# A fused Fourier layer and gated MLP on one core: transposing each half of a tile's rows in one run of four, with the spectral work's plan times moved

## The chip, the cores and the metric

One core of one Trainium2 chip runs the whole program. The metric is the device time of one execution in microseconds (us); the kernel before is given as the median of three runs. One further execution was taken with the hardware profiler, and all rows below come from it. PE is TensorE (matmuls), PEld its weight loads, DVE is VectorE, ACT is ScalarE, POOL is GpSimd and SP the engine that issues most of the DMAs.

## The reference

```python
X = np.fft.rfft(x, axis=1)                       # x: 8 x 3072 x 256
Yr = Xr @ w_r - Xi @ w_i + b_r
Yi = Xr @ w_i + Xi @ w_r + b_i
Y  = softshrink(Yr, 0.01) + 1j * softshrink(Yi, 0.01)
y  = np.fft.irfft(Y, n=3072, axis=1)             # 24576 rows of 256
xn = y / sqrt(mean(y*y) + 1e-6) * rms_g
out = (silu(xn @ w_gate) * (xn @ w_val)) @ w_out # d_ff = 1536
```

## The kernel before, in words

There are eight batches of 3072 rows. Each batch goes through the **spectral work** (a DFT of 3072 points split into 24 x 128, a 256 x 256 mixing product, soft threshold, and the way back) and then through the **MLP**. The spectral work of batch b+1 runs beside the MLP of batch b; that of batch 0 stands alone at the start.

The MLP works on tiles of 512 rows: six per batch, 48 in all, numbered T = 0 to 47. Each tile goes through 12 **steps**, one per block of 128 of the 1536 hidden columns, so a batch is 72 steps. A step makes the gate and value products (`straight`, line 949, for T below 3, and `products`, line 973, with seven products instead of eight, from T = 3 on), the silu and the multiplication on ACT and DVE, and the product with w_out (`down`, line 1016) that adds up in the PSUM bank `acc` over the 12 steps. Every operand is held as two rounded halves (high and low), and each product is three matmuls of 128 x 128 by 128 x 256. All matmuls of the steady part (lines 959, 983, 1018 of the MLP, 572, 611 to 634, 676 to 699 of the spectral work) have this one shape, and come in groups of three or a multiple of it.

**The transposes** (`transposes`, line 912; the matmuls are line 917). Before a tile's first step, its 512 x 256 normalised rows must stand with the 256 columns on the partitions: eight transposes of 128 x 128 per tile on TensorE, four for each half h of the columns. The four of one half go to one PSUM bank of the ring `f`, which has a single bank and which the spectral products `pf`, `pm` and `pb` also take in turn; ACT then copies the bank to `xf` (line 935) or, for T below 3, ACT and DVE copy it to `xn` (lines 930 and 932). For T above 3 the first half (h = 0) is emitted as two pairs: `cut` is 2, a pair is issued, then an operation on a made-up engine "D" that emits nothing and costs 0.8 in the plan, then the other pair. The second half (h = 1) is one run of four. For T = 1 to 3 both halves are runs of four. T = 0 takes its rows from a separate tile.

**What sets the order.** `Plan` (line 128) collects operations with engines, a cost, the tokens they read and write and a due time `at[0]`, counted in steps. `ordered` (line 147) hands out the rooms of each ring in order of due time; `schedule` (line 190) simulates the engines, forward by due time and then, eight times, backward and forward by how late an operation may start, and keeps the best. The instructions are emitted in that order, and each engine works in the order of emission. The constants of lines 35 to 40 are due times: `LATER` (line 1024) is how many steps after its own a step's w_out product is due; `DECODE` (line 1172) moves the decoding of the weight groups 1 to 5, each with one load issued by SP (`weights64`, line 843), two ACT and four DVE operations, and the splitting and storing behind them; `FIRST` and `LATER_ON` (line 1283) say between which steps the three parts of the spectral work of batch 1 and of batches 2 to 7 are spread (lines 1265 to 1275), the table loads of POOL (`load_tab`, line 544) among them; `BACK` is added to all of those.

Of the kernel before, what the change touches and what calls it, by code (L numbers as in the profile page):

```python
# [31 lines left out]
ORDER = [0, 9, 6, 3, 8, 4, 10, 2, 1, 7, 5, 11]  # L32
LAM = 0.01
PLAIN_OF = ()
LATER = 4.67
AHEAD = 60
DECODE = (-7.78, -3.84, -1.42)
BACK = -0.5
FIRST = (21.23, 29.83, 51.87, 60.24)
LATER_ON = (-0.73, 5.35, 42.8, 75.89)  # L40
PLAIN = 3
GE = 9

# [254 lines left out]
def fourier_glu_kernel(ctx: ExitStack, tc: tile.TileContext, x, w_r, w_i, b_r, b_i, wg, wv, wo, rg, tabs, units, tws, out):  # L298
    nc = tc.nc
    B, S, D = x.shape  # L300
    FF = wg.shape[1]
    P = 128
# [35 lines left out]
    def f32(ap):  # L338
        return ap.bitcast(F32)
# [7 lines left out]
    def op(engines, cost, fn, r=(), w=()):  # L347
        plan.add(at[0], engines, cost, fn, [*r, *gate], w)

    def dve(n):  # L350
        return 0.09 + n / 990

    def act(n, more=0.0):
        return 0.1 + more + n / 1180
# [39 lines left out]
    class Bank(Room):  # L394
# [9 lines left out]
        def flat(self):  # L404
            return self().rearrange("p a b -> p (a b)")
# [11 lines left out]
    def load_x(s, n=4):  # L417
        if s.b:
            op("S", 0.01, lambda _: s(), [], s.tok(*range(24)))
        for p in (0, 4, 2, 6)[:8 // n]:  # L420
            for a in range(3):
                slots = range(8 * a + p, 8 * a + p + n)

                def go(_, slots=slots):
                    for p0, p1 in _runs(slots[0], slots[-1] + 1):
                        nc.sync.dma_start(out=s()[:, p0:p1, :], in_=xv[s.b][:, N1[p0]:N1[p1 - 1] + 1:3, :])

                op("S", 2.4 * n / 4, go, [], s.tok(*slots))
# [483 lines left out]
    def transposes(get, toks, T, h, xn, xf):  # L912
        ps = Room("acc" if T == 0 and h else "f", (P, 4, P), f"pt{T}_{h}")

        def go(i0, i1):
            for i in range(i0, i1):
                PE.matmul(  # L917
                    ps()[:, i, :], lhsT=get(i)[:, h * P:(h + 1) * P], rhs=ident,
                    start=(i == 0), stop=(i == 3), is_transpose=True, skip_group_check=True,
                )  # L920

        flat = lambda: ps().rearrange("p a b -> p (a b)")
        cut = 2 if T > PLAIN and not h else 4
        op("P", 0.45 * cut / 4, lambda _: go(0, cut), toks, ps.first)
        if cut < 4:
            op("D", 0.8, lambda _: None, [], [ps.tok])
            op("P", 0.25, lambda _: go(cut, 4), toks, [ps.tok])
        if xf is None:
            to = lambda lp: xn()[:, lp, 2 * h:2 * h + 2, :].rearrange("p a b -> p (a b)")
            op("A", act(512) + 0.09, lambda _: A.activation(to(0), flat(), AF.Copy, scale=rgs[:, h:h + 1]), [ps.tok, "rgs"], [xn.part(f"h{h}0")] + xn.first * (h == 0))  # L930
            w = [xn.part(f"h{h}1")] + ["ready"] * (T == 0 and h)
            op("V", dve(512) + 0.06, lambda _: V.scalar_tensor_tensor(to(1), flat(), rgs[:, h:h + 1], f32(to(0)), ALU.mult, ALU.subtract), [ps.tok, xn.part(f"h{h}0")], w)
            return
        to = lambda: xf()[:, 2 * h:2 * h + 2, :].rearrange("p a b -> p (a b)")
        op("A", act(512) + 0.09, lambda _: A.activation(to(), flat(), AF.Copy, scale=rgs[:, h:h + 1]), [ps.tok, "rgs"], [xf.tok] + xf.first * (h == 0))

    def combine(T, xn, xf):
        x = [(lambda k=k: xf()[:, k, :]) for k in range(7)]
        for o, a, b, f in ((4, 1, 3, ALU.add), (1, 0, 1, ALU.subtract), (5, 4, 0, ALU.subtract), (6, 2, 5, ALU.subtract)):
            add(256, lambda e, o=o, a=a, b=b, f=f: e(x[o](), x[a](), x[b](), f), [], [xf.tok])  # L940
        for k0, k1 in ((0, 2), (4, 6), (2, 4), (6, 7)):
            w = [xn.part(f"h{k0}")] + xn.first * (k0 == 0)
            q = lambda k0=k0, k1=k1: xf()[:, k0:k1]
            op("A", act(256 * (k1 - k0)), lambda _, q=q, k0=k0, k1=k1: A.activation(xn()[:, 0, k0:k1], q(), AF.Copy), [xf.tok], w)
            add(256 * (k1 - k0), lambda f, q=q, k0=k0, k1=k1: f(xn()[:, 1, k0:k1], q(), f32(xn()[:, 0, k0:k1]), ALU.subtract), [xf.tok], w)
# [56 lines left out]
    def step(n, xn, i, mixed):  # L1002
# [20 lines left out]

        at[0] = n + LATER
        for c in range(4):
# [3 lines left out]
    def store(b, t, o):  # L1029
        r = Room("o", (P, 4, D), f"o{b}_{t}")  # L1030
        for k in range(2):
            op("A", act(512), lambda _, k=k: A.activation(r()[:, 2 * k:2 * k + 2], o()[:, 2 * k:2 * k + 2], AF.Copy), [o.tok], [r.tok] if k else r.first)

        def go(_):
            for p0, p1 in _runs(4 * t, 4 * t + 4):
                nc.sync.dma_start(out=ov[b][:, N1[p0]:N1[p1 - 1] + 1:3, :], in_=r()[:, p0 - 4 * t:p1 - 4 * t, :])

        op("S", 1.5, go, [r.tok], [])
# [71 lines left out]
    def bits(g, c):  # L1110
        n = 3 * g + c
        get, tok = (lambda: early()[:, n % 6]), early.tok(*range(4 * (n % 6), 4 * (n % 6) + 4))
        op("S", 2.4, lambda _: weights64(g, c, get()), [], tok)
        w = decode(g, c, get, tok, ("h", "h") if n == 2 else (("G", "xs"), ("z", "F"))[n % 2])
        if c == 0:
            gate_w[0] = w
        elif c == 1:
            up_weights(g, gate_w[0], w)
        else:
            out_weights(g, w)  # L1120
# [44 lines left out]
    for h in range(2):  # L1165
        transposes(lambda i: rows()[:, i, :], [f"{rows.tok}.{p}" for p in range(4)] + [rows.tok, "ident"], 0, h, xns[0], None)

    for g in range(1, NG):
        if g == GE:
            gate.append("ready")  # L1170
        for c in range(3):
            at[0] = 2 * g + DECODE[c]
            bits(g, c)
# [41 lines left out]
    def spectrum(s, times):  # L1215
# [50 lines left out]
        for k in range(3):  # L1266
# [3 lines left out]
            for m, c in zip(mine, cost):  # L1270
                t = times[k] + (times[k + 1] - times[k]) * done / whole
                o = plan.ops[m]
                pace = (f"go{int(t - AHEAD)}",) if t >= AHEAD else ()
                plan.ops[m] = (t + BACK, *o[1:4], o[4] + pace, o[5])
                done += c

    for b in range(B):
        s = seqs[b]
        if b + 1 < B:
            seqs[b + 1] = Seq(b + 1)  # L1280
            at[0] = STEPS * (b - 1) + 60 if b else 10.6
            load_x(seqs[b + 1])
            spectrum(seqs[b + 1], [STEPS * b + t for t in (FIRST if b == 0 else LATER_ON)])
        for t in range(NT):
            T = b * NT + t
            for i in range(NF):
                n = NF * T + i
                if T:
                    at[0] = n - 3
                    if not plain(T):  # L1290
                        trs[n] = fetch(0, i, Room("tr", (P, 2, 512), f"tr{n}", F32R))
                    else:
                        trs[n] = trs[n - 1] if i % 4 else fetch(2, i // 4, Room("tr", (P, 2, 512), f"tb{n}", F32R))
                    if NF <= n < NF * PLAIN and n % (PLAIN - 1) == 0:
                        at[0] = n - 2.9
                        mixed_weights((n - NF) // (PLAIN - 1))
                    at[0] = n - 1
                    wo_s[n] = fetch(1, i, Room("wo", (P, 2, D), f"wo{n}", F32R))
                o = step(n, xns[T], i, not plain(T))
                if i == 0 and T + 1 < NT * B:  # L1300
                    nb, nt = (b, t + 1) if t + 1 < NT else (b + 1, 0)
                    xns[T + 1] = Room("xn", (P, 2, 7, 256), f"xn{T + 1}", F32R)
                    xf = Room("xf", (P, 7, 256), f"xf{T + 1}") if not plain(T + 1) else None
                    for h in range(2):
                        at[0] = NF * (T + 1) - 4 + h
                        transposes(
                            lambda i, nb=nb, nt=nt: seqs[nb]()[:, 4 * nt + i, :],
                            seqs[nb].tok(*range(4 * nt, 4 * nt + 4)), T + 1, h, xns[T + 1], xf,
                        )
                    if xf:  # L1310
                        combine(T + 1, xns[T + 1], xf)
            at[0] = NF * (T + 1) + LATER - 0.95
            store(b, t, o)
# [31 lines left out]
```

## Time and profile before

| | us |
|---|---|
| median of three runs | 2746.87 |
| lowest and highest run | 2743.99, 2752.15 |
| the profiled execution's own time | 2750.04 |
| its span, first to last instruction | 2748.3 |
| mean granted TensorE clock | 0.996 of full speed |

The span is what the rows add up to; the profiled execution's own time is 1.7 us longer, for what lies around the span. It is 3.2 us (0.1%) above the median of the runs.

How to read the rows. A busy time is the union of an engine's instructions. A matmul row gives the duration of one, start to modelled end, which is longer than the distance from one start to the next, since matmuls are pipelined. A window's "(x59)" counts the instructions that lie in it wholly or in part. PEclk is the granted clock of TensorE as a share of full speed.

### The profile page before, as it was taken

The numbers are of one execution on the slowest core, as the hardware profiler recorded it, in microseconds if no ns is written. First come the engines' busy times: TensorE is split into PE (matmuls) and PEld (weight loads), VectorE is DVE, ScalarE is ACT, GpSimd is POOL, SyncE is SP. The second block draws the span as 40 slices with busy tenths as digits, with TensorE's granted clock in tenths as the row PEclk, the third lists the DMA queues.
The fourth block names the chain that finished last, engine by engine and source line by source line (L and its number), as shares of the span: only waits on it lengthen the run. The fifth ranks groups of instructions, "written<-read, shape, count | busy, mean of one in ns | idle before, by whom it ended". The sixth has DMA issues, their size and how long they took to land.

```text
span 2748.3 us, 60168 instructions
## 1 busy us (share of the span) xinstructions
PE 2710.2 (99%) x23321; PEld 2696.1 (98%) x23321; DVE 2322.3 (84%) x4066; ACT 1982.6 (72%) x4891; POOL 90.4 (3%) x177
## 2 busy tenths in 40 slices
PE   7899999999999999999999999999999999999999
PEld 6799999999999999999999999999999999999999
DVE  9989789987998779987899878997789987976665
ACT  4655678777777778777786777877778777776665
POOL 0000000000000000000000000000000000000000
PEclk9999999999999999999999999999999999999999
DMA  6466667676777767767776676766667676666665
GB/s 216 154 223 215 207 220 252 221 230 218 227 253 225 220 221 231 233 226 219 226 254 222 219 226 216 263 215 224 226 222 259 204 230 218 212 205 221 215 218 186
DMA packets 256112, 610.94 MB, mean 222 GB/s; under 512 B 24401, under 2 KB 81106, under 8 KB 255826
## 3 DMA queue, kind: packets, MB, share of 16 engines
q1 hardware_dynamic: 231634, 519.00, 56.7%
q0 software_dynamic: 24192, 88.09, 10.8%
q8 instruction: 183, 3.00, 0.4%
q14 instruction: 103, 0.84, 0.1%
HBM read 567.68 MB, written 39.32 MB: 221 GB/s over the span
## 4 chain that ended last, share of the span: by engine, by line
PE 96%; DVE 2%; DMA 1%; issue 0%; ACT 0%; SPq 0%; ACTq 0%; DVEq 0%
PE acc L1018 28%; PE v L983 27%; PE g L983 20%; PE pf L572 4%; PE pm L634 4%; PE pm L630 2%; PE pb L699 2%; PE pt L917 2%; PE v L959 2%; PE g L959 1%; PE pm L755 1%; PE pb L694 1%; PE pf L733 1%; PE pb L779 1%; PE pm L611 1%; PE pb L676 0%
## 5 line engine op out<-in xcount | busy, mean ns | idle before, releaser
L1018 PE MATMUL acc<-wo,hs 128*128 128x256 f32 x6912 | 1002.5, 278 | 1.9 <-DVE hs L1011 0.8
L1018 PEld LDWEIGHTS acc<-wo,hs 128*128 128x128 f32 x6912 | 884.8, 188 | 2.7 <-DVE hs L1011 1.0
L983 PE MATMUL v<-xn,tr 128*128 128x256 f32 x4860 | 784.0, 279 | 1.3 <-DVE y L996 1.2
L983 PEld LDWEIGHTS v<-xn,tr 128*128 128x128 f32 x4860 | 657.1, 188 | 2.2 <-DVE y L996 1.9
L983 PE MATMUL g<-xn,wb 128*128 128x256 f32 x3240 | 540.7, 278 | 0.0
L996 DVE TENSOR_TENSOR y<-v,p 128x512 f32<-128x512 f32 x540 | 370.8, 687 | 130.2 <-PE v L983 124.8
L1011 DVE TENSOR_TENSOR hs<-h,hs 128x512 fp32r<-128x512 f32 x576 | 394.9, 686 | 81.0 <-ACT hs L1010 77.6
L1010 ACT ACTIVATE hs<-h 128x512 fp32r<-128x512 f32 x576 | 362.0, 628 | 119.6 <-DVE h L1000 63.5
L983 PEld LDWEIGHTS g<-xn,wb 128*128 128x128 f32 x3240 | 446.4, 188 | 0.3
L1000 DVE TENSOR_TENSOR h<-h,y 128x512 f32<-128x512 f32 x540 | 369.8, 686 | 50.6 <-ACT h L999 47.7
L989 ACT ACTIVATE v<-g 128x256 f32<-128x256 f32 x540 | 199.4, 369 | 132.4 <-PE g L983 128.9
L983 PE MATMUL g<-xn,tr 128*128 128x256 f32 x1620 | 274.6, 278 | 0.0
L983 PE MATMUL v<-xn,wb 128*128 128x256 f32 x1620 | 273.7, 278 | 0.0
L992 ACT ACTIVATE v<-v 128x256 f32<-128x256 f32 x540 | 199.9, 371 | 91.0 <-PE v L983 87.5
L999 ACT ACTIVATE h<-v 128x256 f32<-128x256 f32 x540 | 206.5, 382 | 61.9 <-PE v L983 59.0
L997 ACT ACTIVATE h<-g 128x256 f32<-128x256 f32 x540 | 206.3, 382 | 57.3 <-PE g L983 36.7
L983 PEld LDWEIGHTS g<-xn,tr 128*128 128x128 f32 x1620 | 225.3, 188 | 0.1
L983 PEld LDWEIGHTS v<-xn,wb 128*128 128x128 f32 x1620 | 225.2, 188 | 0.0
L545 POOL DMA_DIRECT2D tab<-in_tabs_dram x168 | 89.4, 532 | 2247.4 <-PE pf L572 1180.2
L990 ACT ACTIVATE p<-g 128x256 f32<-128x256 f32 x300 | 114.2, 381 | 40.7 <-DVE y L996 39.8
L572 PE MATMUL pf<-tab,as 128*128 128x256 f32 x1008 | 134.9, 277 | 0.3 <-issue 0.2
L572 PEld LDWEIGHTS pf<-tab,as 128*128 128x128 f32 x1008 | 123.8, 188 | 0.7 <-issue 0.4
(172 smaller groups left out, 3531.9 us busy)
## 6 DMA issues: line engine op xcount, KB each, us to landing
tr<-dt SPq DMA_DIRECT2D x540, 512.0 KB, 4.0
wo<-do SPq DMA_DIRECT2D x564, 256.0 KB, 3.5
tab<-in_tabs_dram POOLq DMA_DIRECT2D x168, 512.0 KB, 4.5
out_dram<-o SPq DMA_DIRECT2D x32, 512.0 KB, 5.4
seq<-in_x_dram SPq DMA_DIRECT2D x28, 512.0 KB, 6.2
seq<-in_x_dram SPq DMA_DIRECT2D x25, 256.0 KB, 4.7
unit<-in_units_dram SPq DMA_DIRECT2D x12, 512.0 KB, 4.3
dt<-tw SPq DMA_DIRECT2D x12, 512.0 KB, 5.7
```

The lines of the kernel that those rows point to most:

```text
L572: PE.matmul(ps[:, h, :], lhsT=r()[:, lp, ri, h * P:(h + 1) * P], rhs=f[:, rp, ri, :], start=(h + k + ri == 0), stop=(k == 2 and ri == 1), ...
L983: PE.matmul(dst(), lhsT=w(lp), rhs=xn()[:, rp, x, :], start=start and k == 0, stop=k == 2, skip_group_check=True)
L989: op("A", act(256), lambda _: A.activation(left(), p1(), AF.Copy), [one.tok], two.first)
L990: op("AV", {"A": act(256), "V": dve(256)}, lambda e: A.activation(p5(), p5_(), AF.Copy) if e == "A" else V.tensor_copy(p5(), p5_()), [one. ...
L992: op("A", act(256), lambda _: A.activation(right(), left(), AF.Copy), [], [two.tok])
L996: op("V", dve(512), lambda _: V.tensor_tensor(y(), two(), p5().unsqueeze(1).to_broadcast([P, 2, 256]), ALU.add), [two.tok, p5.tok], y.first)
L997: op("A", act(256), lambda _: A.activation(s()[:, :256], p1(), AF.Silu), [one.tok], s.first)
L999: op("A", act(256), lambda _: A.activation(s()[:, 256:], right(), AF.Silu), [two.tok], [s.part("b")])
L1000: op("V", dve(512), lambda _: V.tensor_tensor(s(), s(), y().rearrange("p a b -> p (a b)"), ALU.mult), [y.tok, s.part("b")], [s.tok])
L1010: op("A", act(512), lambda _: A.activation(h()[:, 0], s(), AF.Copy), [s.tok], h.first)
L1011: add(512, lambda f: f(h()[:, 1], s(), f32(h()[:, 0]), ALU.subtract), [s.tok], [h.tok])
L1018: PE.matmul(o()[:, c, :], lhsT=h()[:, lp, c * P:(c + 1) * P], rhs=wo_()[:, rp, :], start=(i == 0 and k == 0 and c % 2 == 0), stop=(i == NF ...
```

## The change

Both halves of each tile are now transposed in one run of four; the two pairs, and the planned pause between them, are gone. For T = 1 to 3 nothing is different in this function, as `cut` was 4 there. Six planning constants have other values.

```diff
-LATER = 4.67
+LATER = 4.77
 AHEAD = 60
-DECODE = (-7.78, -3.84, -1.42)
-BACK = -0.5
-FIRST = (21.23, 29.83, 51.87, 60.24)
-LATER_ON = (-0.73, 5.35, 42.8, 75.89)
+DECODE = (-6.74, -4.23, -1.63)
+BACK = -0.63
+FIRST = (17.81, 28.26, 48.79, 59.49)
+LATER_ON = (-3.72, 6.26, 39.96, 69.5)
...
-        def go(i0, i1):
-            for i in range(i0, i1):
+        def go(_):
+            for i in range(4):
                 PE.matmul(
                     ps()[:, i, :], lhsT=get(i)[:, h * P:(h + 1) * P], rhs=ident,
                     start=(i == 0), stop=(i == 3), is_transpose=True, skip_group_check=True,
                 )
...
-        cut = 2 if T > PLAIN and not h else 4
-        op("P", 0.45 * cut / 4, lambda _: go(0, cut), toks, ps.first)
-        if cut < 4:
-            op("D", 0.8, lambda _: None, [], [ps.tok])
-            op("P", 0.25, lambda _: go(cut, 4), toks, [ps.tok])
+        op("P", 0.45, go, toks, ps.first)
```

## Rows read from the trace of the kernel before

**Rows 1.** The page, part 1: busy time, share of the span and instructions of each engine.
```profile
PE 2710.2 (99%) x23321; PEld 2696.1 (98%) x23321; DVE 2322.3 (84%) x4066; ACT 1982.6 (72%) x4891; POOL 90.4 (3%) x177
```
**Rows 2.** Waits of TensorE, longest first: us in total, times, longest.
```profile
PE warm L1082 <- DMA seq<-in_x_dram: 11.6, 1, 11.6
PE pt L917 <- ACT rows L822: 11.0, 1, 11.0
PE pf L733 <- DVE seq L464: 2.9, 1, 2.9
...
```
**Rows 3.** Windows, TensorE alone: stretch, us, PE busy (count), PEclk, DMA share, GB/s.
```profile
0.00:118.00 118.00, 91.65 (x507) 0.93 0.65 211
118.00:343.00 225.00, 220.56 (x1887) 1.00 0.61 198
343.00:2690.00 2347.00, 2345.05 (x20469) 1.00 0.69 226
2690.00:2748.30 58.30, 52.98 (x466) 0.97 0.54 182
```
**Rows 4.** The chain that ended last: start, us, what (merged).
```profile
33.35 3.45 PE pm L755 x16
...
241.20 1.36 PE pf L572 x12
...
258.15 1.41 PE pf L572 x12
```
**Rows 5.** Windows between the runs of transposes of T = 1 to 4.
```profile
144.10:150.50 6.40, 6.40 (x59) 1.00 0.75 259
151.50:171.40 19.90, 19.90 (x178) 1.00 0.80 254
172.10:185.90 13.80, 13.80 (x120) 1.00 0.60 201
186.70:194.70 8.00, 8.00 (x71) 1.00 0.92 332
239.40:243.60 4.20, 4.20 (x39) 1.00 0.72 212
244.40:334.40 90.00, 90.00 (x766) 1.00 0.63 203
...
353.10:361.20 8.10, 8.10 (x74) 1.00 0.52 174
```
**Rows 6.** Windows between the runs of the last two tiles.
```profile
2615.00:2630.30 15.30, 15.30 (x133) 1.00 0.63 221
...
2635.20:2661.00 25.80, 25.80 (x230) 1.00 0.63 215
2661.50:2676.80 15.30, 15.30 (x132) 1.00 0.69 232
...
2681.70:2741.00 59.30, 59.30 (x526) 1.00 0.59 200
```
**Rows 7.** The transposes' tile pt: duration ns min/median/max, first and last start.
```profile
L917 PE MATMUL pt<-ident,seq x376: 270/272/273, 143.3 to 2681.2; 128*128 128x128 f32 x188
L935 ACT ACTIVATE xf<-pt,rgs x90: 663/682/701, 239.5 to 2681.7; 128x512 f32<-128x512 f32 x90
```
**Rows 8.** Timeline of TensorE at a pair and at a run of four: start, us.
```profile
2630.41 0.38 PE L917 MATMUL pt<-ident,seq 128*128 128x128 f32 x2
...
2630.98 0.75 PE L983 MATMUL v<-xn,tr 128*128 128x256 f32 x5
...
2634.52 0.60 PE L917 MATMUL pt<-ident,seq 128*128 128x128 f32 x4
...
2635.31 0.50 PE L1018 MATMUL acc<-wo,hs 128*128 128x256 f32 x3
```
**Rows 9.** The page, part 6: DMA issues, count, KB each, us to landing.
```profile
tab<-in_tabs_dram POOLq DMA_DIRECT2D x168, 512.0 KB, 4.5
seq<-in_x_dram SPq DMA_DIRECT2D x28, 512.0 KB, 6.2
```

## The prediction

> **What bounds the kernel now.** I read four views, in this order. The page's busy times come first: TensorE is busy for 99% of the span, DVE for 84%, ACT for 72% [rows 1]. The waits of TensorE say whether that is real: its longest three, 25.5 us together, belong to the start, where the first rows land and the first tile is normalised [rows 2]. The windows then show that from 343 to 2690 us it sits idle for only 2347.00 - 2345.05 = 1.95 us [rows 3]. So nothing that another engine does sooner can shorten this stretch; only the number of TensorE's instructions, and the distance from one to the next, can.
>
> That distance has **two values**, and this is what the reader should see. In the chain of work that ended last, the same twelve `pf` matmuls take 1.36 us at 241 us and 1.41 us at 258 us [rows 4]: 113.3 and 117.5 ns each. The windows give it more finely. A matmul's modelled duration (276 to 281 ns) reaches back over the edge of a window, so a window counts about 2.4 too many; 90.00 us with 766 matmuls is 90.00/763.6 = 117.8 ns [rows 5], and 59.30 us with 526 is 113.3 ns [rows 6]. I call them the fast and the slow pace: 113.3 and 117.8 ns, 4.5 ns apart. The granted clock reads 1.00 in all these windows, DMA share and bytes are alike, and no wait stands there: neither the clock nor a late operand makes the slow pace. What changes at the edges of these windows is a **run of transposes** [rows 5, 6].
>
> How much is slow: 20469 matmuls at 113.3 ns would need 2319.8 us (113.33 taken) of the 2347.0 [rows 3]. The difference is 27.2 us, 1.95 of it idle; the other 25.2 us, at 4.5 ns each, are 5,600 slow matmuls, 27% of the stretch. (Transposes count as matmuls here; the next part shows that they cost about the same.)
>
> **The change part by part.**
>
> *The transposes themselves.* 376 of them serve T = 1 to 47 [rows 7], before and after. From the start of a pair to the fourth matmul start behind it 0.57 us pass, of which three matmul distances at the slow pace are 0.353: the pair costs 0.22. A run of four: 0.79 less three fast distances, 0.34, is 0.45 [rows 8]. Two pairs or one run: 0.44 against 0.45, 44 times, is nothing (-0.5 to +0.5 us).
>
> *The bank.* Before, ACT could copy the first half only after the second pair, some 15 us after the first pair in the last tiles (15.3 us is the slow window between them) [rows 6]. Now it can do so right behind the run, in 0.68 us [rows 7], so ring `f` comes free sooner for the spectral products. Those do not hold TensorE up in the steady part, whose idle time is 1.95 us in all [rows 3]; taken as 0, with -2 us as the most it could give. The planned pause emits no instruction: 0.
>
> *The pace behind each run.* This is the term that decides. There are 44 tiles with two runs of four each in place of a pair, a pair and a run. What the trace shows:
> - A pair met at the fast pace leaves the slow one: the last two tiles have 133 and 132 matmuls in 15.3 us between their pairs, where the fast pace would give 137 [rows 6].
> - The run of four that ends such a tile leaves the fast pace: 230 in 25.8 us and 526 in 59.3 us [rows 6], as it does at T = 4 [rows 5]. All 44 do so in the timeline, of which the first and the last windows are shown.
> - But none of these 44 runs follows a run of four; a pair is always in between. Runs of four alone are shown only by T = 1 to 3. A window's count tells the pace: after the six runs, 59 (fast would be 58.9, slow 56.7), 178 (178, 171), 120 (124, 119.5), 71 (73, 70.3), 39 (39.5, 38) and 766 (797, 766) [rows 5]: fast, fast, slow, slow, fast, slow. The fourth run met the slow pace and left it; the fifth came behind a stall of the start. The last slow stretch lasts 90 us, until a pair and a run of four come.
>
> So the nearest rows for the new pattern, runs of four behind runs of four, end slow in three of six cases. The bounds are: every run ends fast, 0 slow matmuls, -25.2 us; every run ends slow, 20469 x 4.5 = 92.1 us, +66.9 us. I take half, by those six: 10,234 x 4.5 = 46.1 us, less the 25.2 paid now, **+20.9 us**.
>
> The Trainium skill, page "TensorE: Matmul & The Clock Gate", section "LDWEIGHTS (loading the stationary operand)", gives the time of a weight load by its columns alone, about 128/1.2 = 107 ns by my estimate, whatever ran before. By that rule there is one pace, and this term is 0 instead of +20.9. The two paces at a clock of 1.00 speak against it [rows 5], but it is a rival below.
>
> *The moved plan times.* `LATER` puts each w_out product 0.1 step later, and with it the stores, issued by SP, by 0.1 step: an order of work among products that are all waiting, 0. `DECODE` moves, for weight groups 1 to 5, the load on SP's queue, two ACT and four DVE operations and the splitting behind them by +1.04, -0.39 and -0.21 step; `FIRST` starts the next batch's spectral work 3.42 steps sooner. Both fall in the stretch from 118 to 343 us, where TensorE is idle for 225.00 - 220.56 = 4.4 us [rows 3]. All of that gone is -4.4; as much again is +4.4; nothing in the rows says which, so 0. `LATER_ON` and `BACK` start the spectral work of batches 2 to 7 about 3 steps sooner and end it 6.5 steps sooner. Its table loads go out on POOL's queue (168 of them, landing in 4.5 us), and the loads of x on SP's keep their due time [rows 9]. DVE and ACT have 16% and 28% to spare [rows 1], and the cover is that TensorE always has MLP products ready; were it gone, the price is the fourth rival's. 0.
>
> **The sum.** 2750.0 (the profiled execution) + 20.9 = 2770.9. That execution lies 3.2 us over the median of the runs, so on the median's scale 2767.7, say **2768 us**.
>
> **The rivals.**
>
> *Every run of four ends fast* (the other side: faster). For it: all 44 runs of four from T = 4 on do, from either pace, and 25.8 and 59.3 us at 113.3 ns follow in the last two tiles [rows 6]. If what matters is the run's own length, and T = 1 to 3 are disturbed by the start, then taking the pairs away takes the slow stretches away. It shows from where under 18% of the matmuls are slow (18% is 16.6 us, 8.6 less than now). Time: 2750.0 - 25.2 = 2724.8, on the median's scale 2722. Against it: the slow stretch of 90 us that began behind a run of four with no stall before it [rows 5]. Chance 0.30.
>
> *Nothing changes.* Either the pace is not the transposes' doing, or the new mixture is again near 27% slow (18 to 36%: -9 to +8 us). Time 2747. The change not doing what it says belongs here too: the four are issued by one function call, so they cannot be drawn apart, but with one bank in ring `f` the second run still waits for ACT's copy of the first, and the two halves may end up as they were. Chance 0.12.
>
> *The clock falls behind a longer run.* At the start, where the granted clock averages 0.93 over 118 us [rows 3], sixteen matmuls took 3.45 us, 216 ns each [rows 4], the lower level of 1.2 GHz, twice the 113.3. If each of the 88 runs of four and the three matmuls behind it, 0.79 us [rows 8], went at that level, each would take 0.79 us longer, +70 us: 2750.0 + 70 - 3.2 = 2817. Against it: 50 runs of four stand in this trace and the clock reads 1.00 from 118 to 2690 us [rows 3]. Chance 0.01.
>
> *The spectral work's earlier start makes DVE late at a batch's edge.* The next batch's first sums would then stand in DVE's queue ahead of the MLP's multiplications while a load of x, 6.2 us, is under way [rows 9]. Six edges x 6.2 us is +37 us at most: 2784. It decides once TensorE's waits on DVE at 343 us and every 330 us after sum to over 8 us; they are under 2 now [rows 3]. Chance 0.04.
>
> **How the numbers follow.** The forecast, that a good part of the runs of four leave the slow pace, has 0.53. About 0.3%, 8 us, is what a measurement of this kernel can tell from no change. Slower by more: 0.53 + 0.01 + 0.04 = 0.58. Faster by more: 0.30. Within: 0.12. The forecast begins at 37% slow: 34.1 - 25.2 = +8.9, on the median's scale 2756. At 83% slow it is 76.4 - 25.2 = +51.2, there 2798, and 2800 with 2 for the plan times. So its own range is 2756 to 2800. The range for 8 in 10 takes in the fast rival and the first 2 us of its plan-time bound: 2720 to 2800; the clock and the all-slow end (2814) are left out.
>
> **What would show it.** Right: windows between the runs of the last tiles with 117.8 ns between matmuls, also behind runs of four; TensorE's count per 330 us falling; mean matmul durations nearer 281 than 276 ns; clock 1.00; waits as now. Wrong: 113.3 ns from run to run (then the fast rival), or new waits of TensorE on DVE at the edges of batches.

## The result and the profile after

The changed kernel takes **2774.27 us** (median of 4 runs, 2773.16 to 2775.29) against 2747.74 for the kernel before (4 runs): 26.5 us more, a ratio of 1.0096 with a 95% interval of 1.0078 to 1.0113. The forecast was 2768, with a range of 2720 to 2800. The profiled execution of after took 2773.16 us, its span is 2771.4.

Busy times of after (the page, part 1), the line that answers to [rows 1]:

```profile
PE 2733.7 (99%) x23321; PEld 2720.0 (98%) x23321; DVE 2330.5 (84%) x4063; ACT 1987.4 (72%) x4894; POOL 90.4 (3%) x177
```

TensorE issues the same 23321 matmuls and is busy 23.5 us longer: that is the whole growth of the span (2771.4 - 2748.3 = 23.1). Its waits in after, in the columns of [rows 2]:

```profile
PE warm L1078 <- DMA seq<-in_x_dram: 11.6, 1, 11.6
PE pt L917 <- ACT rows L822: 11.0, 1, 11.0
PE pf L733 <- DVE seq L464: 2.2, 1, 2.2
PE pf L572 <- ACT as L564: 1.5, 1, 1.5
...
PE acc L1014 <- ACT o L1028: 0.7, 4, 0.2
```

The two longest are equal and none of the others is long enough to matter. The last line shown is new, 0.7 us in four waits: at four edges between batches the first w_out product waits for the copy of the bank `acc`. The windows of TensorE in after, in the columns of [rows 3]:

```profile
0.00:118.00 118.00, 91.64 (x524) 0.96 0.66 211
118.00:343.00 225.00, 221.02 (x1901) 0.99 0.62 202
343.00:2690.00 2347.00, 2344.87 (x20239) 1.00 0.69 224
```

The third line is the result. In the same 2347 us TensorE is as busy as before (2344.87 against 2345.05 us), at the same clock and with the same DMA share, and finishes 230 matmuls fewer. I call **slow time** what a kernel's busy time in this stretch has over 113.33 ns for each matmul counted: 2344.87 - 20239 x 0.11333 = 51.2 us here, 25.3 us before [rows 3]. It has grown by 25.9 us. At 4.5 ns each that is 11,400 slow matmuls, 56% of them, where there were 27%. Slow time also holds what a wait costs beyond the idle time that the profile shows, because a matmul's modelled duration (276 ns) reaches 163 ns past the next start: at the wait of 0.18 us at 1106.62 us in after, two distances are 455 and 223 ns, 0.45 us more than two fast ones. So a share of slow matmuls worked out "by the row" is an upper figure; counted one by one from the starts in the trace, 55% of the distances are at the slow pace in after and 25% before.

Windows between the runs of four of the last tiles of after, in the columns of [rows 6]:

```profile
2543.30:2589.80 46.50, 46.50 (x413) 1.00 0.68 227
2590.60:2609.60 19.00, 19.00 (x164) 1.00 0.64 222
2610.40:2637.30 26.90, 26.90 (x231) 1.00 0.58 202
2638.20:2656.40 18.20, 18.20 (x163) 1.00 0.68 229
2657.20:2684.10 26.90, 26.90 (x230) 1.00 0.62 211
2684.90:2704.00 19.10, 19.10 (x165) 1.00 0.64 211
2704.90:2764.00 59.10, 59.10 (x524) 1.00 0.60 201
```

With 2.4 taken from each count, as in the prediction, the distances are 113.2, 117.6, 117.7, 113.3, 118.2, 117.5 and 113.3 ns. Two stretches at about 117.8 ns follow one at 113.3 ns, then one at 113.3 ns comes again: **each run of four here moves the pace on by one place in a cycle of three**. In [rows 6] a pair began a slow stretch and the run of four behind it ended it; here a slow stretch lasts from one run of four to the next but one.

The transposes' own rows in after, in the columns of [rows 7], show that they did not change:

```profile
L917 PE MATMUL pt<-ident,seq x376: 270/272/273, 142.4 to 2704.4; 128*128 128x128 f32 x188
L931 ACT ACTIVATE xf<-pt,rgs x90: 671/690/709, 246.1 to 2704.8; 128x512 f32<-128x512 f32 x90
```

### The profile page after: what moved, and what is told of

The parts are those of the page before. It is cut to its first block, busy times and chain, and to the rows that moved or that the text cites. A ratio compares the mean times of both kernels' runs of the same rounds, so it can differ in the third digit from the quotient of the medians.

```text
span 2771.4 us, 60161 instructions
## 1 busy us (share of the span) xinstructions
PE 2733.7 (99%) x23321; PEld 2720.0 (98%) x23321; DVE 2330.5 (84%) x4063; ACT 1987.4 (72%) x4894; POOL 90.4 (3%) x177
## 4 chain that ended last, share of the span: by engine, by line
PE 97%; DVE 2%; DMA 1%; ACT 1%; issue 0%; SPq 0%; ACTq 0%; DVEq 0%
PE acc L1014 28%; PE v L979 27%; PE g L979 20%; PE pf L572 4%; PE pm L634 4%; PE pb L699 2%; PE pm L630 2%; PE v L955 2%; PE g L955 2%; PE pt L917 2%; PE pm L755 1%; PE pb L694 1%; PE pb L779 1%; PE pm L611 1%; PE pf L733 1%
```

## The experiments

Each line of windows below is TensorE's from 343 to 2690 us, in the columns of [rows 3], and each slow time is worked out from it as above. A measured ratio is against the kernel before, measured beside it, with its 95% interval.

**1 and 2: the shape and the plan times, one at a time.** The first keeps the runs of four and puts the six planning constants back; the second keeps the new constants and puts the pairs back.

```diff
...
-FIRST = (17.81, 28.26, 48.79, 59.49)
-LATER_ON = (-3.72, 6.26, 39.96, 69.5)
+FIRST = (21.23, 29.83, 51.87, 60.24)
+LATER_ON = (-0.73, 5.35, 42.8, 75.89)
...
```

> The kernel before with the runs of four alone; the plan times stay the old ones. Theory A (the runs' shape sets the pace: met by runs of four alone, the pace goes fast, slow, slow, fast from run to run): 45 to 65% of the matmuls at 117.8 ns, 2762 to 2785 us. Rival B (the moved plan times cost the 26 us): 27% slow as before, 2740 to 2755 us.

Measured: 2781.08 us, ratio 1.0122 (1.0106 to 1.0138).

```profile
343.00:2690.00 2347.00, 2341.23 (x20141) 1.00 0.68 223
```

```diff
...
-        op("P", 0.45, go, toks, ps.first)
+        cut = 2 if T > PLAIN and not h else 4
+        op("P", 0.45 * cut / 4, lambda _: go(0, cut), toks, ps.first)
+        if cut < 4:
+            op("D", 0.8, lambda _: None, [], [ps.tok])
+            op("P", 0.25, lambda _: go(cut, 4), toks, [ps.tok])
```

> The changed kernel's plan times with the old pairs. Theory A: 25 to 32% of the matmuls slow, 2740 to 2757 us. Rival B: 2766 to 2782 us, or waits of TensorE that the kernel before does not have.

Measured: 2756.17 us, ratio 1.0030 (1.0017 to 1.0044).

```profile
343.00:2690.00 2347.00, 2343.00 (x20452) 1.00 0.69 226
```

The slow time is 58.7 us with fours and the old times, 25.2 with pairs and the new times. So theory A's ranges hold in both, and B's in neither: the shape of the runs makes the loss, +33 us of slow time by itself (with it the plan also orders the other matmuls anew; experiment 3 does not). The plan times then took 6.8 us off again (2781.08 to 2774.27): with the runs in other places the slow time is 51.2 instead of 58.7 us, and idle time 2.1 instead of 5.8. With pairs the new times cost 9 us at the median. The row explains 2 of these (idle 4.00 against 1.95 us, a few short waits, far from the 26 us that B needed); the profiled execution took 2753.42, and the seven runs spread from 2749.30 to 2758.87, so the rest stays open.

**3: runs of six.** The first two transposes of each run are written twice from T = 1 on, 188 more in all.

```diff
-            for i in range(4):
+            run = ([0, 1, 2, 3] * 3)[:2] * (T > 0)
+            for k, i in enumerate(run + [0, 1, 2, 3]):
...
```

> The changed kernel with two transposes written twice, so that every run of T = 1 to 47 is six long: 188 more transposes at 0.11 us are +21 us. Theory A in its sharper form (each transpose moves the pace on by one of three places, so a run moves it by its length modulo three): a run of six leaves the pace that it meets, the pace changes only at stalls, the slow 53 us go; 2740 to 2755 us and under 15% slow. Rival C (any run of some length upsets the pace, two of three behind it are slow): 2790 to 2800 us.

Measured: 2751.99 us, ratio 1.0020 (1.0010 to 1.0030).

```profile
343.00:2690.00 2347.00, 2344.18 (x20586) 1.00 0.69 226
```

188 transposes were added, 20.5 us at 109 ns each, and the kernel is 22.3 us faster than after. The slow time fell to 11.2 us. This settles that the transposes steer the pace: nothing else was touched. In the trace the other 22,937 matmuls of TensorE stand in the same order as in after, and the runs at the same places among them; the same holds for experiments 6, 7, 10 and 12. That the count goes modulo three was the theory of this moment; the next runs ended it.

**4 and 5: all eight in one run, with one repeated (nine) and without (eight).** The second half's four go to a bank of the ring `gb`, and the run is placed eight steps later in the listing. The diff is of the eight; the nine has `* 1` for `* 0`.

```diff
+            work = [(h, i) for i in range(4)] if not T else [(0, 0)] * 0 + [(k, i) for k in range(2) for i in range(4)]
+            for m, (k, i) in enumerate(work):
...
-        op("P", 0.45, go, toks, ps.first)
+        if not T:
+            op("P", 0.45, go, toks, ps.first)
+        elif not h:
+            op("P", 0.9, go, toks, banks[0].first + banks[1].first)
...
-                if i == 0 and T + 1 < NT * B:
+                if i == NF - 4 and T + 1 < NT * B:
...
+                    banks = [Room(tag, (P, 4, P), f"pt{T + 1}_{k}") for k, tag in enumerate(("f", "gb"))]
```

> The changed kernel with all eight transposes of a tile of T = 1 to 47 in one run into two banks, and one written twice: runs of nine, 47 more transposes, +5 us. Theory A, sharper form: nine is a multiple of three, the pace stays fast; 2722 to 2735 us, under both kernels. Rival C: two of three runs leave it slow, 2775 to 2785 us. The bank taken from the gate products' ring may add a few us of waits of TensorE in either case.

Measured: 2819.57 us, ratio 1.0263 (1.0247 to 1.0278).

```profile
343.00:2690.00 2347.00, 2341.01 (x19888) 1.00 0.68 220
```

> All eight transposes of a tile in one run with none repeated (second half of rows into a bank of the g ring, the run moved to the same place as in the run of nine). With every matmul at 113.3 ns this kernel would take about 2720 us, with every one at 117.8 ns about 2815. Theory L (a long run, over six, drops TensorE to the slow pace and holds it there, as the run of nine did): over 75% of the matmuls slow, 2795 to 2820 us. Rival M (the runs count up to six: six is nothing, four goes around in three, so eight counts as two and goes around in three; nine was an odd one): two thirds slow, a fast tile and two slow ones by turns, 2770 to 2790 us. Rival E (the repeated transpose of the run of nine did the harm, even runs of six and more keep the pace): under 15% slow, 2715 to 2735 us.

Measured: 2815.98 us, ratio 1.0246 (1.0231 to 1.0262).

```profile
343.00:2690.00 2347.00, 2340.19 (x19887) 1.00 0.68 220
```

Both theories of the fourth run fell: nine is three times three, and TensorE is at the slow pace nearly throughout. Eight does the same, with nothing repeated, so the repeated transpose was not the cause. Slow time is 87.1 and 86.4 us; the all-slow bound of the prediction, 92.1, is nearly reached. Theory L is right for these two lengths. That the length alone does it is not shown, since the run's place, the second bank and the order of the other matmuls changed with it; but experiment 11, with the same place and bank, is mostly fast. In the run of nine the granted clock also fell to 0.50 once, from 352.5 to 362.8 us, amid three waits of TensorE of 0.6 to 1.1 us: 35 matmuls, some 4 of its 87.1 us.

**6 and 7: runs of five and of seven.** As the third run, with `[:1]` and `[:3]` in place of `[:2]`.

> The changed kernel with the first transpose of each run written twice: two runs of five for every tile. 94 transposes more are about 10 us. Theory E (an odd run drops the pace and never gives it back, as nine did; even ones of six and over keep it): over 75% slow, 2805 to 2830 us. Rival M (counting up to six: five goes around in six runs, fast once): five of six slow, 2795 to 2815 us, with fast stretches in a regular cycle. Rival K (from five on a run keeps the pace, until it is too long): under 15% slow, 2725 to 2745 us, which would beat the kernel before.

Measured: 2737.52 us, ratio 0.9965 (0.9951 to 0.9979): **faster than both kernels**, with 94 transposes more.

```profile
343.00:2690.00 2347.00, 2345.00 (x20639) 1.00 0.70 227
```

> The changed kernel with the first three transposes of each run written twice: two runs of seven for every tile, 282 transposes more, about 32 us. Theory E (odd runs hold the slow pace): over 75% slow, 2825 to 2850 us. Rival M (counting up to six: seven is one): five of six slow, 2815 to 2840 us. Rival K (runs of five to seven keep the pace): under 15% slow, 2745 to 2765 us.

Measured: 2770.66 us, one run.

```profile
343.00:2690.00 2347.00, 2345.16 (x20536) 1.00 0.70 224
...
2587.60:2606.90 19.30, 19.30 (x166) 1.00 0.66 220
2607.80:2633.80 26.00, 26.00 (x231) 1.00 0.60 204
2634.80:2654.00 19.20, 19.20 (x165) 1.00 0.66 219
2655.00:2681.00 26.00, 26.00 (x232) 1.00 0.66 217
```

Five keeps the fast pace: slow time 6.0 us. Seven turns it at every run: the four windows, between the last runs, are 118.0, 113.7, 118.1 and 113.2 ns. It happens that the stretches at the slow pace are the short ones, so its slow time is only 17.8 us; the 282 added transposes, 30.7 us, make the rest of its time. None of the three theories had this for seven; for five K was right.

**8: one run of four for each tile**, from the fifth tile on. The second half's transposes are left out there, and both copies read the first half's bank.

```diff
...
-        ps = Room("acc" if T == 0 and h else "f", (P, 4, P), f"pt{T}_{h}")
+        if h == 0 or T <= PLAIN:
+            ps = Room("acc" if T == 0 and h else "f", (P, 4, P), f"pt{T}_{h}")
+            lone[0] = ps
+        else:
+            ps = lone[0]
...
-        op("P", 0.45, go, toks, ps.first)
+        if h == 0 or T <= PLAIN:
+            op("P", 0.45, go, toks, ps.first)
```

> The changed kernel with the transposes of the second half of the rows left out from the fifth tile on: both copies read the first half's bank, so those rows' second halves of the features are wrong copies of the first. One run of four is left for each tile, some 180 transposes fewer (about 20 us). Theory of the cycle (each run of four takes the pace one step on, fast, slow, slow, fast, whatever tile or half it belongs to): a fast tile, then two slow ones, by turns, about 60 to 67% of the matmuls slow between the stalls at a batch's edge, 2750 to 2770 us. Rival (the two runs of one tile act together, one lowers the pace and the other gives it back, so a lone run leaves one pace): either under 15% slow, 2700 to 2715 us, or over 85% slow, 2775 to 2800 us.

Measured: 2753.82 us, one run. The windows between its last runs, and the stretch:

```profile
343.00:2690.00 2347.00, 2345.31 (x20255) 1.00 0.70 226
...
2479.90:2524.40 44.50, 44.50 (x395) 1.00 0.67 226
2525.20:2571.50 46.30, 46.30 (x396) 1.00 0.62 213
2572.30:2618.60 46.30, 46.30 (x396) 1.00 0.63 213
2619.30:2663.90 44.60, 44.60 (x395) 1.00 0.67 220
```

113.3, 117.6, 117.6, 113.6 ns: in these last tiles the cycle of three goes by whole tiles, and the time is in that theory's range (55% slow by the row, a little under it). So the cycle does not need a tile's two halves. It is not strict, though: over the whole kernel 13 of the 29 runs met at the fast pace end fast (the table below), some of them without a wait ahead. Some 393 equal matmuls take 44.5 us in one tile and 46.3 in the next, with operands of the same shapes and the same clock.

**9: runs of five with the plan times of before.**

```diff
...
-LATER_ON = (-3.72, 6.26, 39.96, 69.5)
+LATER_ON = (-0.73, 5.35, 42.8, 75.89)
...
+            run = ([0, 1, 2, 3] * 3)[:1] * (T > 0)
...
```

> Two runs of five for every tile with the plan times of the kernel before. Theory (the run's length sets the pace, a run of five keeps the fast one wherever it falls, and the plan times only move where runs fall): under 10% of the matmuls slow, as with the new plan times; 2731 to 2741 us, level with the 2737.5 of the runs of five with the new times. Rival (the plan times have a price of their own, as the pairs with the new times showed, which took 9 us more although fewer of their matmuls were slow): the old times then give that back here, 2722 to 2730 us, at the same share of slow matmuls.

Measured: 2740.71 us, ratio 0.9972 (0.9962 to 0.9982).

```profile
343.00:2690.00 2347.00, 2341.80 (x20561) 1.00 0.70 226
```

The theory's range of times holds, and the rival's does not: 13% of the matmuls are slow by the row, but counted one by one 5%, as the theory said (the rest is what its waits cost beyond their idle time), and with the pace kept the two sets of plan times are 3.2 us apart, the old ones the slower, with 3.2 us more idle time (5.2 against 2.0). The intervals overlap. The 9 us of the second run are not a price of the new times in general.

**10: a short fifth.** The repeated transpose takes 32 rows and 32 columns.

```diff
...
+                m = 32 if k < len(run) else P
                 PE.matmul(
-                    ps()[:, i, :], lhsT=get(i)[:, h * P:(h + 1) * P], rhs=ident,
+                    ps()[:, i, :m], lhsT=get(i)[:m, h * P:(h + 1) * P], rhs=ident[:m, :m],
...
```

> As the runs of five with the new plan times, but the transpose that is repeated takes only 32 rows and 32 columns of its operand (it is overwritten by the whole one behind it), so the run has five instructions and about the time of four and a quarter. Theory N (the number of transposes in a run sets the pace): under 15% slow, and the extra transpose nearly free, 2725 to 2736 us. Rival D (the time that the run takes sets the pace: this run is nearer to one of four): the pace goes around as in runs of four, 40 to 65% slow, 2755 to 2785 us.

Measured: 2763.66 us, ratio 1.0057 (1.0042 to 1.0072).

```profile
343.00:2690.00 2347.00, 2345.45 (x20432) 1.00 0.70 225
```

One of its runs in the timeline, and then a run of five of the sixth experiment between the same neighbours (start, us, engine line op):

```profile
2690.26 0.50 PE L1016 MATMUL acc<-wo,hs 128*128 128x256 f32 x3
2690.69 0.83 PE L919 MATMUL pt<-ident,seq 32*128 32x32 f32 x5
2691.28 0.60 PE L981 MATMUL v<-xn,tr 128*128 128x256 f32 x3
2691.71 0.50 PE L1016 MATMUL acc<-wo,hs 128*128 128x256 f32 x3
```

```profile
2667.22 0.51 PE L1015 MATMUL acc<-wo,hs 128*128 128x256 f32 x3
2667.57 0.71 PE L918 MATMUL pt<-ident,seq 128*128 128x128 f32 x5
2668.03 0.60 PE L980 MATMUL v<-xn,tr 128*128 128x256 f32 x3
2668.47 0.50 PE L1015 MATMUL acc<-wo,hs 128*128 128x256 f32 x3
```

On the pace theory N is right: behind the runs it stays fast, as the table below counts. On the price it is wrong: from one `acc` group to the next 1.45 us pass, against 1.25. The short transpose costs 0.20 us more than the whole one it replaces, 19 us over 94 runs, and that is most of the 26 us between the two kernels. So the time lies in rival D's range, but not for D's reason: one by one, 10% of the distances are slow. The slow time of this row (29.9 us) holds those 19 too.

**11: five and three.** The second half's first transpose joins the first half's run, into a bank of `gb`; none is repeated. Otherwise as the run of eight: the runs stand at its place in the listing.

```diff
...
+            work = [(h, i) for i in range(4)] if not T else [(1, i) for i in range(1, 4)] if h else [(0, i) for i in range(4)] + [(1, 0)]
...
```

> The tile's eight transposes as a run of five (the first half's four and the second half's first, that one into a bank of the g ring) and a run of three, none repeated. A run of three has not been seen. Theory (a short run met at the fast pace lowers it, as the pair did in the kernel before and the four does in this one; five gives it back or keeps it): slow from each run of three to the next run of five, over 70% slow, 2790 to 2815 us. Rival (three keeps the pace as five does): under 15% slow, 2720 to 2735 us, the fastest of all, unless the bank of g that is held longer stalls TensorE, which would show as waits of its v or g on the copies.

Measured: 2749.87 us, ratio 1.0011 (1.0001 to 1.0020).

```profile
343.00:2690.00 2347.00, 2339.54 (x20410) 1.00 0.69 225
```

Neither: 26.5 us of slow time, 29% of the matmuls by the row, and idle time of 7.5 us. Three met at the fast pace mostly kept it, so the theory's ground is gone. Counted one by one, 16% of the distances are slow; the rest of the slow time is in what the waits cost beyond their idle time and in 6.8 us at a granted clock of 0.50, from 349.5 us on. The 5 us of idle time over after's 2.1 are not the longer-held bank that the rival feared: none of the waits that the profile lists (6.7 us) is on a copy of that bank, and 5.7 of the 7.5 us stand between 343 and 460 us.

**12: four, then five.** As the sixth run, with `(T > 0 and h)`: only the second run of a tile has a repeated transpose.

> The changed kernel with a repeated transpose in the second run of each tile alone: four, then five. Theory (five always ends fast, whichever pace it meets; four met fast always ends slow): slow between a tile's first run and its second and nowhere else. In the runs of five these stretches sum to 384 us, about 3,300 matmuls, 15%; at 4.45 ns each 14.5 us over the some 2721 us of an all-fast kernel, and 47 transposes more, some 5 us: 2736 to 2748. Rival (five only keeps the pace that it meets, as six mostly did): the fours alone turn the pace then, fast, slow, slow, fast over three tiles, 55 to 70% of the matmuls slow, 2775 to 2795 us.

Measured: **2734.15 us**, ratio 0.9951 (0.9935 to 0.9968), the fastest of all. Its stretch and the windows between its last runs:

```profile
343.00:2690.00 2347.00, 2343.55 (x20624) 1.00 0.70 227
...
2573.40:2598.80 25.40, 25.40 (x226) 1.00 0.61 207
2599.80:2618.00 18.20, 18.20 (x163) 1.00 0.70 230
2619.40:2644.80 25.40, 25.40 (x226) 1.00 0.68 223
2645.70:2663.90 18.20, 18.20 (x163) 1.00 0.67 220
```

All four windows are at 113.3 to 113.6 ns, also those of 18.2 us, which stand behind a run of four that met the fast pace. Slow time is 6.2 us. Both theories let such a four end slow; it nearly never does here. The time is 2 us under the range of the theory, whose slow stretches behind the fours are missing.

**All runs of transposes together.** Counted from the starts in the traces, T = 1 to 47: the pace just ahead of a run, and the mean distance from the 6th to the 12th matmul behind it. Counting farther would mix in something else: at four batch edges a wait breaks in at the 13th. Experiments 2 and 11 are left out.

| kernel, length of run | fast to fast | fast to slow | slow to slow | slow to fast |
|---|---|---|---|---|
| before, 2 | 2 | 40 | 25 | 21 |
| before, 4 | 25 | 2 | 1 | 22 |
| after, 4 | 8 | 31 | 29 | 26 |
| experiment 1, 4 | 6 | 31 | 27 | 30 |
| experiment 8, 4 (one a tile) | 13 | 16 | 11 | 10 |
| experiment 12, 4 | 45 | 1 | 0 | 1 |
| experiment 12, 5 | 46 | 0 | 0 | 1 |
| experiment 6, 5 | 91 | 0 | 0 | 3 |
| experiment 9, 5 | 91 | 0 | 0 | 3 |
| experiment 10, 5 (one short) | 89 | 0 | 0 | 5 |
| experiment 3, 6 | 85 | 0 | 3 | 6 |
| experiment 7, 7 | 0 | 45 | 2 | 47 |
| experiment 5, 8 | 0 | 10 | 37 | 0 |
| experiment 4, 9 | 0 | 6 | 37 | 4 |

A run of four met at the fast pace ends slow in after and fast in experiment 12 and before. Fifteen runs of four that met the fast pace in both after and experiment 12 ended slow in the one and fast in the other, at the same places in the same order of matmuls. So the length of a run, the pace ahead of it and its neighbours do not fix the pace behind it: TensorE carries something else from run to run that the profile does not show. After's own trace says the same. The short waits at four edges of batches meet a slow stretch and leave a fast one; the next run of four is met fast and ends fast (1170.66 us is the first), and only the one after it begins the cycle again. The other four of its eight runs from fast to fast are two behind stalls of the first 350 us and two with no wait ahead (148.28 and 842.70 us).

## Why the prediction was right

**What bounds the kernel** held. TensorE's idle time from 343 to 2690 us is 2.13 us, was 1.95; the time came from the distance between its matmuls and from nothing else.

**The transposes themselves, 0**: right. Their durations are the same 270/272/273 ns as in [rows 7].

**The bank, 0**: right. Idle time in the stretch did not fall.

**The pace behind each run, +20.9**: the mechanism was right, the size short. The step was "I take half, by those six". The slow time rose from 25.3 to 51.2 us, so the term is +25.9, 56% slow. The six runs of T = 1 to 3 were disturbed by stalls of the start; without stalls two stretches in three are slow, which at equal lengths would be 67%, and the stalls at the batches' edges bring back a fast stretch of some length. That the sum came so near is in part luck: by the shape of the runs alone the term was +33 us (experiment 1), and the moved plan times, put at 0, took 7 back. [rows 5] hold the sequence fast, slow, slow, fast once, and do not show that it repeats.

**The moved plan times, 0**: right in what was argued, and not the whole of it. From 118 to 343 us TensorE's idle time is 3.98 us, was 4.4. But plan times also set how many matmuls lie between one run and the next, and so how long a slow stretch is: with runs of four the move was worth -6.8 us (experiment 1). The sum had no term for that.

**The sum.** Forecast +20.9; measured +26.5 by the medians. The pace's term is 5.0 short; the rest, 0.6, is within the spread of the runs.

**The rivals.** *Every run of four ends fast* fell: 31 of the 39 that were met fast ended slow. Its ground, that all 44 such runs of before leave the fast pace, was true, but those all followed a pair. *Nothing changes* fell with the ratio's interval. *The clock* stays at 1.00 in after from 207 to 2770 us, through 90 runs of four; it is 0.50 once behind the start, from 203.7 to 207.1 us, after TensorE's waits and with no run of transposes near, and the fall in experiment 4 also came amid waits. That rival's price was misread as well: the sixteen matmuls at 33.35 us took 216 ns each in a stretch whose granted clock is 1.00 (33.4 to 36.8 us), so they do not show the lower level; in after, at 0.50, the distance is 213 ns. *DVE late at a batch's edge*: the waits there are on ACT, 0.7 us in all. The rule of the Trainium skill, page "TensorE: Matmul & The Clock Gate", section "LDWEIGHTS (loading the stationary operand)", by which one pace would do, does not settle the distance here: some 393 equal pairs of load and matmul take 44.5 or 46.3 us in experiment 8, and the loads' own rows last 188 ns in the mean in after, not the 107 ns estimated from that rule.

**How far the measure carries.** From after, the time of each other kernel should differ by its slow time, its idle time and 109 ns for each transpose added (from its start to the fourth matmul start behind it a run of five takes 2668.47 - 2667.57 = 0.90 us under experiment 10, one of four 0.79 [rows 8]). Experiment 4: 35.9 + 3.9 + 5.1 = +44.9, 2819.2 against 2819.57 measured. Experiment 6: -45.2 - 0.1 + 10.2 = -35.1, 2739.2 against 2737.52. Experiment 7: -33.4 - 0.3 + 30.7 = -3.0, 2771.3 against 2770.66. Experiment 12: -45.0 + 1.3 + 5.1 = -38.6, 2735.7 against 2734.15. The worst are experiment 9, 7.3 us over the measured time, and experiment 2, 6.0 under it. This is an account of where the time lies, not a second proof: slow time is itself worked out from the profile of the same kernel.

**What stays open.** That the runs of transposes steer the pace is shown: experiments 3, 6, 7 and 12 change nothing else, and the order of the other matmuls is the same. Why a matmul has two distances, and what is carried from run to run, is not. The same page says, in the section "Back-to-back issue gap", that the spacing is set by load and matmul together through a reorder window of 64 entries; no run here shows what stands in such a window.

## What to carry to other kernels

In a stretch where an engine is never idle, divide its busy time by its instructions, stretch by stretch, and compare equal instructions: a busy share of 99% hid 25 us before the change and 51 after. When two values appear, look at what stands at the edges between them, and try its neighbours (one instruction more or fewer) before explaining it: one repeated transpose for each tile, 5 us of work, was worth 40 us here against after, and 13.8 us against the kernel before. Such a gain hangs on the whole order of the instructions, so measure it again after each change of plan.

## What was not expected of the hardware

- TensorE has two steady paces for the same load and matmul at a granted clock of 1.00, 113.3 and 117.8 ns, and holds either for hundreds of matmuls (at the fast pace 524 are counted in the last window of after, at the slow one 766 in [rows 5]).
- Behind a run of five transposes TensorE was at the fast pace in 94 of 94 cases (experiment 6), behind a run of eight in 0 of 47. Time does not grow with the number of transposes: five in a run are 36.8 us faster than four.
- A short wait can turn the pace, and either way. In after four waits of 0.18 us at batches' edges met the slow pace and left the fast one, but one of 0.17 us at 440.1 us met the fast pace and left the slow one.
- A transpose of 32 x 32 among ones of 128 x 128 costs 0.20 us more than another of 128 x 128, in each of 94 runs.
